# Loading two quarters of a weight in column halves, and trying more plans, in a fused attention and MoE kernel that plans its own instruction order

## The chip, the cores and the metric

The kernel runs on 1 core of one Trainium2 chip. The metric is device time in microseconds (us).

PE is TensorE (PEld its weight loads), DVE is VectorE, ACT is ScalarE, POOL is GpSimd, SP is SyncE.

## The reference, cut to what matters

```python
# q, k, v: (8 batches, 8 heads, 576, 64) float32; attention in a window of +-32 positions
scores = where(abs(i - j) <= 32, q @ k.T / 8, -1e9)
attn_out = softmax(scores) @ v
x = attn_out.transpose(0, 2, 1, 3).reshape(4608, 512)     # one row per token
h = x @ w_in            # (512, 2048)
g = relu(h) ** 2
out = g @ w_out         # (2048, 512), float32 out
```

## The kernel before

The kernel is a generator. It records every operation with what it reads and writes, an estimated duration and a key; then it plans an order for all five engines with a model of its own, several times over with different offsets, keeps the plan that its model likes best, and emits that order with the semaphore waits that it needs. So a change of the loads also changes the order of everything else.

The tokens are worked in 9 tiles of 512. For the first tile the first product is cut into 16 units: token group g (128 tokens) by weight quarter q (512 of the 2048 columns of w_in). A unit is 16 matmuls of 128 columns. It may start when the attention result of its group and its quarter are there.

```python
MORE = (-1000, -500, 0, 500, 1000, 1500)          # offsets that are tried on modelled landings
ORDER = ("k01 q01 v00 v01 v02 k03 q03 v03 k04 q04 w10 w11 v04 w12 w13 k05 q05 k10 q10 v10 k11 q11 v11 "
         "w20 w21 w22 w23 k12 q12 v12 k13 q13 v13 k14 q14 v14").split()    # POOL's loads, in order

def load_w1(self, d, key):                        # a quarter of w_in, float32 in HBM, cast to bf16
    src = self.w_in[:, 512 * d:512 * d + 512].rearrange("(f p) c -> p f c", p=128)
    self.p.rec("POOL", lambda e: e.dma_start(self.W1[:, :, 512 * d:512 * d + 512], src),
               writes=[("w1", d)], dma=(f"w1{d}", 0), key=key, dur=770, move=(32, 82, 500 if d > 1 else 1300))

def mm1_small(self, T, g, q, key):                # one unit of the first product
    ...
    def f(e):
        for d in range(4 * q, 4 * q + 4):
            for ft in range(4):
                mm = e.matmul(ht[:, 128 * (d % 4):128 * (d % 4) + 128], self.W1[:, ft, 128 * d:128 * d + 128],
                              self.XT[:, ft, t0:t0 + 128], start=(ft == 0), stop=(ft == 3))
        return mm
    first = self.p.rec("PE", f, reads=[("xt", 8 * T + 2 * g), ("xt", 8 * T + 2 * g + 1), ("w1", q)],
                       writes=[("ht", k % 2), ("mo", k)], key=key, dur=900)
    ...

def mm2(self, T, u, seg, key):                    # second product: a quarter (seg) of w_out, one output bank
    x = 4 * T + u
    gt, op, tag = self.GT[T % 2], self.OUTP[x % 2][:], ("outp", x % 2)    # two output banks in all
    ...                                           # reads ("w2", seg)

# schedule(): for every offset in MORE and every margin, plan; keep the best by the model
    for pad, more in [(p, m) for p in PADS for m in MORE]:
        ...
        if best is None or s < best[0]:
            best = (s, out, start, end, T)
```

A name like `w10` is quarter 0 of w_in, `w23` is quarter 3 of w_out, `v04` is piece 4 of v of batch 0, `k12` is piece 2 of k of batch 1. All these loads cast float32 to bf16 and go through one queue, that of POOL.

The softmax here doesn't subtract the row's maximum and nothing guards it: scores larger than these inputs give would overflow.

## Time and profile before

| | before |
|---|---|
| device time, median of 3 runs | 299.93 us (299.88 to 300.82) |
| span of the profiled run | 297.6 us |
| PE busy | 289.7 us, 97% |
| packets in POOL's queue | 113120 |
| first MoE matmul | 17.37 us |
| last w_out quarter lands / is first used | 41.1 / 41.4 us |

A line of the timeline has the start, the duration, the engine, the line of the kernel, the operation and its operands; in brackets is how long the engine idled before and what ended that. An issue line of a DMA ends with the microseconds from issue to landing.

### The profile page before, as it was taken

What the parts mean: (1) busy time and instruction counts of PE and PEld (TensorE: products, weight loads), DVE (VectorE), ACT (ScalarE), POOL (GpSimd) and SP (SyncE); (2) the same over time, 40 slices, a digit from 0 to 9 for tenths busy, and PEclk for the clock granted to TensorE, in tenths of its full rate; (3) what the DMA queues carried; (4) which work ended last, traced back from release to release, by engine and by line L of the source; (5) the groups of instructions that cost most, each with busy time, mean ns of one, the idle gap of its engine ahead of it and who ended that gap; (6) DMA issues with size and microseconds to landing.
All of it is one profiled execution on the core that took longest, in us unless ns stands there. A gap on an engine that the chain in (4) does not pass through costs nothing.

```text
span 297.6 us, 6577 instructions
## 1 busy us (share of the span) xinstructions
PE 289.7 (97%) x2669; PEld 167.1 (56%) x2705; DVE 174.9 (59%) x407; ACT 160.9 (54%) x265; POOL 105.7 (36%) x131
## 2 busy tenths in 40 slices
PE   8989999999999999999999999999999999999996
PEld 4679855867678754454444454545454544444445
DVE  4865764774989974787565756845554862222200
ACT  2856534657668646573656465546564654444411
POOL 8999841432435514540445424325410000000000
PEclk9999999999999999999999999999999999999999
DMA  9999999999999999999999999999993030100122
GB/s 156 169 201 169 207 172 193 177 157 157 160 175 187 128 183 144 143 150 158 149 109 164 160 151 133 108 171 121 166 119 98 9 82 36 37 35 35 37 89 88
DMA packets 166814, 39.30 MB, mean 132 GB/s; under 512 B 157824, under 2 KB 162304, under 8 KB 166784
## 3 DMA queue, kind: packets, MB, share of 16 engines
q0 software_dynamic: 113120, 17.90, 90.5%
q1 hardware_dynamic: 46512, 11.15, 27.8%
q10 hardware_dynamic: 7152, 9.83, 9.6%
q8 instruction: 21, 0.34, 0.4%
q14 instruction: 9, 0.07, 0.1%
HBM read 36.70 MB, written 9.44 MB: 155 GB/s over the span
## 4 chain that ended last, share of the span: by engine, by line
PE 89%; POOL 4%; DMA 4%; issue 1%; ACT 0%; DVE 0%; POOLq 0%
PE outp L935 40%; PE ht L883 28%; PE ht L865 7%; PE ht L842 5%; DMA qraw<-in_q_dram 4%; PE sc L719 3%; PE sc L663 3%; POOL vx L546 1%; POOL kraw L480 1%; POOL w L568 1%; PE sc L506 1%; POOL qraw L480 1%; PE sc L911 1%; PE outp L911 1%; PE sc L767 0%
## 5 line engine op out<-in xcount | busy, mean ns | idle before, releaser
L935 PE MATMUL outp<-w,gt 128*128 128x512 bf16 x535 | 132.0, 379 | 1.6 <-issue 0.5
L898 DVE TENSOR_TENSOR gt<-rt 128x512 bf16<-128x512 bf16 x144 | 59.5, 419 | 63.4 <-ACT rt L889 55.5
L883 PE MATMUL ht<-xt,w 128*128 128x512 bf16 x373 | 93.4, 379 | 0.8 <-issue 0.2
L889 ACT ACTIVATE rt<-ht 128x512 bf16<-128x512 f32 x96 | 57.2, 599 | 61.3 <-PE ht L883 58.8
L935 PEld LDWEIGHTS outp<-w,gt 128*128 128x128 bf16 x560 | 53.0, 98 | 59.2
L883 PEld LDWEIGHTS ht<-xt,w 128*128 128x128 bf16 x384 | 36.4, 98 | 41.5
L480 POOL DMA_DIRECT2D qraw<-in_q_dram x39 | 34.3, 881 | 50.9 <-PE ht L883 28.1
L480 POOL DMA_DIRECT2D kraw<-in_k_dram x39 | 34.4, 882 | 38.2 <-PE ht L883 18.7
L546 POOL DMA_DIRECT2D vx<-in_v_dram x40 | 35.7, 894 | 23.2 <-PE ht L883 10.7
L942 ACT ACTIVATE oe<-outp 128x512 f32<-128x512 f32 x35 | 20.9, 598 | 28.1 <-PE outp L935 28.1
L684 ACT ACTIVATE e<-sc 128x1024 bf16<-128x1024 f32 (+1 forms) x38 | 31.7, 875 | 7.3 <-PE sc L663 7.3
L700 DVE TENSOR_TENSOR pt<-e,mask 128x512 bf16<-128x512 bf16 (+1 forms) x63 | 29.6, 507 | 9.4 <-ACT e L684 9.1
L743 DVE TENSOR_TENSOR xr<-pf,rs 128x512 bf16<-128x512 f32 (+1 forms) x42 | 27.4, 681 | 0.3
L842 PE MATMUL ht<-xt,w 128*128 128x128 bf16 x384 | 23.9, 219 | 0.8 <-DMA w<-in_moe_w_in_dram 0.8
L865 PE MATMUL ht<-xt,w 128*128 128x256 bf16 x192 | 23.3, 273 | 0.0
L842 PEld LDWEIGHTS ht<-xt,w 128*128 128x128 bf16 x384 | 21.7, 98 | 1.5 <-DMA w<-in_moe_w_in_dram 0.9
L736 DVE COPY pf<-sc 128x520 f32<-128x520 f32 x21 | 14.7, 698 | 8.9 <-PE sc L719 8.6
L865 PEld LDWEIGHTS ht<-xt,w 128*128 128x128 bf16 x192 | 17.9, 98 | 3.1 <-DMA xt<-xr 0.2
L850 ACT ACTIVATE rt<-ht 128x512 bf16<-128x512 f32 x24 | 14.3, 598 | 9.5 <-PE ht L842 9.2
L738 DVE TENSOR_TENSOR pf<-pf 64x520 f32<-64x520 f32 x21 | 14.7, 698 | 5.9 <-ACT pf L733 5.2
L733 ACT ACTIVATE pf<-sc 128x520 f32<-128x520 f32 x21 | 12.6, 601 | 9.6 <-PE sc L719 8.9
L871 ACT ACTIVATE rt<-ht 128x512 bf16<-128x512 f32 x24 | 14.4, 599 | 6.3 <-PE ht L865 5.0
(85 smaller groups left out, 174.7 us busy)
## 6 DMA issues: line engine op xcount, KB each, us to landing
out_dram<-oe ACTq DMA_DIRECT2D x35, 256.0 KB, 2.9
kraw<-in_k_dram POOLq DMA_DIRECT2D x30, 128.0 KB, 5.2
qraw<-in_q_dram POOLq DMA_DIRECT2D x30, 128.0 KB, 5.2
vx<-in_v_dram POOLq DMA_DIRECT2D x24, 128.0 KB, 5.5
w<-in_moe_w_in_dram POOLq DMA_DIRECT2D x4, 512.0 KB, 10.2
w<-in_moe_w_out_dram POOLq DMA_DIRECT2D x4, 512.0 KB, 16.5
vx<-in_v_dram POOLq DMA_DIRECT2D x16, 96.0 KB, 5.6
xt<-xr SPq DMA_TRANSPOSE x36, 4.0
```

The source lines that it names most:

```text
L480: self.p.rec("POOL", lambda e: e.dma_start(dst, src), writes=[("fraw", b, t, x)], old=[("fraw", b - 2, t, y + (b == 2))], reads=self.pace( ...
L546: self.p.rec("POOL", lambda e: e.dma_start(self.VX[b % 2][r:r + n, s, :, 0:64], self.v[b, :, t0:t0 + n, :].rearrange("h p d -> p h d")), w ...
L684: self.p.rec("ACT", lambda e, d=dst, a=src: e.activation(d, a, ACTF.Exp, scale=0.125), reads=["s" + x for x in ("AC", "BD")[h]], writes=[( ...
L700: self.p.rec("DVE", lambda e: e.tensor_tensor(pt, ee, mb, ALU.mult), reads=[("e", g // 2)] + rd, writes=[("ptt", k)], old=old, key=key + k ...
L743: self.p.rec("DVE", lambda e, w=w, np=np: e.tensor_tensor(bass.AP(self.XR, 512 * (2 * y + w), [[2048, np], [64, 2], [128, 4], [1, 64]]), b ...
L842: mm = e.matmul(ht[:, 128 * (d % 4):128 * (d % 4) + 128], self.W1[:, ft, 128 * d:128 * d + 128], self.XT[:, ft, t0:t0 + 128], start=(ft == ...
L865: mm = e.matmul(ht[:, 256 * (d % 2):256 * (d % 2) + 256], self.W1[:, ft, 128 * d:128 * d + 128], self.XT[:, ft, 64 * s0:64 * s0 + 256], st ...
L883: mm = e.matmul(ht[:], self.W1[:, ft, 128 * d:128 * d + 128], self.XT[:, ft, 512 * T:512 * T + 512], start=(ft == 0), stop=(ft == 3))
L889: self.p.rec("ACT", lambda e: e.activation(rt[:], ht[:], ACTF.Relu), reads=[("ht", k % 2)], writes=[("rt", k % 4)], key=key, dur=560)
L898: self.p.rec("DVE", lambda e: e.tensor_tensor(g, r, r, ALU.mult), reads=[("rt", k % 4)], writes=tags, key=key, dur=430)
L935: mm = e.matmul(op, gt[:, d, 128 * u:128 * u + 128], self.W2[:, d, :], start=(d == 0), stop=(d == 15))
L942: self.p.rec("ACT", lambda e: e.activation(oe[:], op, ACTF.Copy), reads=[tag], writes=[("oe", x % 4)], key=key, dur=560)
```

## The change

Its intent: the first unit waits 0.9 us for quarter 0 of w_in. Loaded in two halves of 256 columns, the first half is there earlier, and the units of the first two token groups are cut so that 8 of their 16 matmuls can run on it. The set of offsets that the planner tries grows from 6 to 13.

```diff
+CUT = 2
-MORE = (-1000, -500, 0, 500, 1000, 1500)
+MORE = (-1500, -1000, -750, -500, -250, 0, 250, 500, 750, 1000, 1250, 1500, 2000)
     def load_w1(self, d, key):
-        src = self.w_in[:, 512 * d:512 * d + 512].rearrange("(f p) c -> p f c", p=128)
-        self.p.rec("POOL", ... writes=[("w1", d)], dma=(f"w1{d}", 0), key=key, dur=770, move=(32, 82, 500 if d > 1 else 1300))
+        parts = 2 if d < CUT else 1
+        w = 512 // parts
+        for h in range(parts):
+            lo = 512 * d + w * h
+            src = self.w_in[:, lo:lo + w].rearrange("(f p) c -> p f c", p=128)
+            self.p.rec("POOL", ... writes=[("w1", d, h)],
+                       dma=(f"w1{d}{h}", 0), key=key + 0.4 * h, dur=770, move=(32, 82, 500) if parts == 1 else (32, 43, 1300))
     # mm1_small
+        if T == 0 and q < CUT and g < 2:
+            for h in range(2):
+                op = self.p.rec("PE", lambda e, h=h: f(e, range(4 * q + 2 * h, 4 * q + 2 * h + 2)), reads=xs + [("w1", q, h)],
+                                writes=[("ht", k % 2)] + ([("mo", k)] if h else []), key=key, dur=450)
     ...                                  # the other readers wait for both halves
```

More of the change, by code (lines that the diff above doesn't have):

```diff
@@ L566, in load_w1 @@
     def load_w1(self, d, key):
-        src = self.w_in[:, 512 * d:512 * d + 512].rearrange("(f p) c -> p f c", p=128)
-        self.p.rec("POOL", lambda e: e.dma_start(self.W1[:, :, 512 * d:512 * d + 512], src),
-                   writes=[("w1", d)], dma=(f"w1{d}", 0), key=key, dur=770, move=(32, 82, 500 if d > 1 else 1300))
+        parts = 2 if d < CUT else 1
[3 more added lines that the diff above has]
+            src = self.w_in[:, lo:lo + w].rearrange("(f p) c -> p f c", p=128)
+            self.p.rec("POOL", lambda e, lo=lo, src=src: e.dma_start(self.W1[:, :, lo:lo + w], src), writes=[("w1", d, h)],
+                       dma=(f"w1{d}{h}", 0), key=key + 0.4 * h, dur=770, move=(32, 82, 500) if parts == 1 else (32, 43, 1300))
     def load_w2(self, d, key):
@@ L837, in mm1_small, with f @@
         t0 = 512 * T + 128 * g
-        def f(e):
-            for d in range(4 * q, 4 * q + 4):
+        def f(e, ds):
+            for d in ds:
                 for ft in range(4):
@@ L844, in f @@
             return mm
-        first = self.p.rec("PE", f, reads=[("xt", 8 * T + 2 * g), ("xt", 8 * T + 2 * g + 1), ("w1", q)], writes=[("ht", k % 2), ("mo", k)], key=key,
-                   dur=900)
-        if not k:
-            self.p.first = first
+        xs = [("xt", 8 * T + 2 * g), ("xt", 8 * T + 2 * g + 1)]
+        if T == 0 and q < CUT and g < 2:
+            for h in range(2):
+                op = self.p.rec("PE", lambda e, h=h: f(e, range(4 * q + 2 * h, 4 * q + 2 * h + 2)), reads=xs + [("w1", q, h)],
+                                writes=[("ht", k % 2)] + ([("mo", k)] if h else []), key=key, dur=450)
+                if not k and not h:
+                    self.p.first = op
+        else:
+            op = self.p.rec("PE", lambda e: f(e, range(4 * q, 4 * q + 4)), reads=xs + [("w1", q, h) for h in range(2 if q < CUT else 1)],
+                            writes=[("ht", k % 2), ("mo", k)], key=key, dur=900)
+            if not k:
+                self.p.first = op
         self.p.rec("ACT", lambda e: e.activation(rt[:], ht[:], ACTF.Relu), reads=[("ht", k % 2)],
@@ L867, in f @@
             return mm
-        self.p.rec("PE", f, reads=[("xt", s0 + u) for u in range(4)] + [("w1", q // 2)], writes=[("ht", k % 2), ("mo", k)],
+        self.p.rec("PE", f, reads=[("xt", s0 + u) for u in range(4)] + [("w1", q // 2, h) for h in range(2 if q // 2 < CUT else 1)], writes=[("ht", k % 2), ("mo", k)],
                    key=key, dur=870)
@@ L885, in f @@
             return mm
-        self.p.rec("PE", f, reads=[("xt", 8 * T + j) for j in range(8)] + [("w1", d // 4)], writes=[("ht", k % 2), ("mo", k)],
+        self.p.rec("PE", f, reads=[("xt", 8 * T + j) for j in range(8)] + [("w1", d // 4, h) for h in range(2 if d // 4 < CUT else 1)], writes=[("ht", k % 2), ("mo", k)],
                    key=key, dur=854)
```

## The prediction

> **What bounds the kernel now.** I read the page first, then the windows table, then the timeline of the first 44 us, then the issues of the weight loads one at a time. First the page:
>
> ```profile
> span 297.6 us, 6577 instructions
> PE 289.7 (97%) x2669; PEld 167.1 (56%) x2705; DVE 174.9 (59%) x407; ACT 160.9 (54%) x265; POOL 105.7 (36%) x131
> ...
> DMA  9999999999999999999999999999993030100122
> ...
> q0 software_dynamic: 113120, 17.90, 90.5%
> ...
> PE 89%; POOL 4%; DMA 4%; issue 1%; ACT 0%; DVE 0%; POOLq 0%
> ```
>
> PE is busy in 97% of the span and carries 89% of the chain of waits; only a DMA and the load issues on POOL take its place, and only early. So the end moves if PE idles less or starts real work sooner, nothing else. The windows table (stretch, length, busy time of PE, PEld, DVE, ACT, POOL) says where PE idles:
>
> ```profile
> 13.40:17.37 3.97, 2.91 (x72) 2.07 (x65) 3.40 (x10) 3.02 (x4) 3.97 (x7) 1.00 1.25 207
> 17.37:20.00 2.63, 2.44 (x45) 2.30 (x46) 1.17 (x3) 1.26 (x3) 2.63 (x4) 1.00 1.52 193
> 20.00:26.50 6.50, 6.34 (x117) 6.13 (x118) 3.65 (x9) 4.36 (x8) 6.50 (x9) 1.00 1.65 187
> 26.50:36.00 9.50, 9.45 (x166) 8.81 (x166) 6.70 (x18) 5.65 (x11) 8.92 (x11) 1.00 1.63 190
> 36.00:50.00 14.00, 13.89 (x138) 7.51 (x140) 7.89 (x17) 5.53 (x10) 5.26 (x6) 1.00 1.94 189
> ```
>
> Before 17.37 PE idles 3.97 - 2.91 = 1.06 us and also runs fillers on zeros (0.53 and 0.38 us). From 20 to 50 it idles 0.16 + 0.05 + 0.11 = 0.32 us in all. From 50 to 250 the same view sums to about 2.1 us, and some of that is missing matmul records (535 of 560 for the second matmul). So about 2 us could be had before 20 us and about 2 us in the other 230.
>
> The timeline shows what the early wait is for (start, duration, engine, line, operation; idle time and its releaser in brackets):
>
> ```profile
> 9.68 1.57 POOL L568 DMA_DIRECT2D w<-in_moe_w_in_dram  x2
> ...
> 16.38 0.38 PE L430 MATMUL outp<-zz 128*128 128x512 bf16 x1
> ...
> 17.36 0.90 PEld L842 LDWEIGHTS ht<-xt,w 128*128 128x128 bf16 x16 [0.92 <-DMA w<-in_moe_w_in_dram]
> ...
> 19.98 1.05 PE L842 MATMUL ht<-xt,w 128*128 128x128 bf16 x16 [0.19 <-DMA w<-in_moe_w_in_dram]
> ...
> 40.54 2.75 PE L935 MATMUL outp<-w,gt 128*128 128x512 bf16 x12
> ...
> 42.46 0.60 ACT L942 ACTIVATE oe<-outp 128x512 f32<-128x512 f32 x1 [1.12 <-PE outp L935]
> ```
>
> The first MoE unit starts when quarter 0 of w_in lands (17.3 us) and the third when quarter 1 lands (19.8 us). Then the issue lines for single loads, the first w_in quarter and the last w_out quarter (the last column is us from issue to landing):
>
> ```profile
> w<-in_moe_w_in_dram POOLq DMA_DIRECT2D x1, 512.0 KB, 7.6
> ```
>
> ```profile
> w<-in_moe_w_out_dram POOLq DMA_DIRECT2D x1, 512.0 KB, 19.2
> ```
>
> Issued at 9.68, quarter 0 lands at 9.68 + 7.6 = 17.28. In the same way the other w_in quarters land at 19.8, 23.0 and 25.6. The w_out quarters, issued at 19.71, 20.45, 21.19 and 21.93 with 13.8, 15.6, 17.5 and 19.2 us to landing, come at 33.5, 36.1, 38.7 and 41.1. POOL issues in 0.75 us what the queue needs 2.6 us to move, so the queue is a backlog up to 42 us.
>
> That last landing matters most. The 12 matmuls at 40.54 are three groups of four, 0.86 us each: w_out quarter 2 for one token block, then quarter 3 for two. The first use of quarter 3 is therefore at 40.54 + 0.86 = 41.4 us, 0.3 us after it lands. The ACT line agrees: its result is evacuated at 42.46, after PE has finished at about 42.3. In the same way quarters 0, 1 and 2 are used 1.9, 1.3 and 0.7 us after they land. The slack shrinks along the row: **PE runs into the queue at 41 us.**
>
> **What the Trainium skill says.** "DMA: Bandwidth & Descriptors", Specifications, gives 512 B as the smallest transfer at line rate. A half quarter has rows of 256 columns, 512 B in bf16: just at that limit. No row of before has that size, so this trace neither agrees nor disagrees; it shows only 1 KB and 128 B packets. The same page, "Issuing engines are not separate DMA queues", says that all issuers share the 16 engines; the backlog of before agrees. The page "TensorE: Matmul & The Clock Gate", "Wait — 56ns, not 53.3ns?", gives 56 ns between 128-column matmuls; the chain shows 0.89 us for 16 of them, 56 ns. So a half unit of 8 is 0.45 us.
>
> **The change part by part.** (1) Two loads of 512 KB become four of 256 KB. PE now waits for halves, and the units of token groups 0 and 1 with quarters 0 and 1 are each recorded as two halves of 8 matmuls. No matmul is added or removed; four more PE waits and two more POOL issues are. POOL: 2 x 0.75 = 1.5 us more of issuing, all in front of a backlog of 7 to 19 us, so it reaches nobody.
>
> (2) The queue. Between 14.5 and 17.2 us only weights moved: 547 packets in 2.7 us on 16 engines, 79 ns for one of 1 KB. Between 17.5 and 19.8 us, 772 small and 334 large packets moved: 2300 - 334/16 x 79 = 650 ns for 48 small ones per engine, 13.5 ns each. A straight line through 128 B at 13.5 and 1 KB at 79 gives an overhead of some 4 ns a packet. Halving turns 512 packets per quarter into 1024, 32 more per engine: 32 x 4 = 0.13 us a quarter, 0.26 us for two. This estimate takes 512 B to be on that line. All later loads of the queue land 0.26 us later: w_out quarter 3 at about 41.4 us. The queue's count should be 113120 + 1024 + 2 x 16 = 114176, the 32 being completion packets (126 issues x 16 = 2016 account for what the data rows leave over).
>
> (3) The first units. Half 0 of quarter 0 should land at 17.28 - 1.31 + 0.07 = 16.05, half 1 at 17.4, the halves of quarter 1 at 18.8 and 20.1. Laying out PE with the measured pieces (transposes 0.25, attention 0.25, half 0.45): unit 0 half 0 at 16.1, in what was filler and idle time; half 1 from 17.4 to 17.85; transpose and attention to 18.4; unit 1 to 19.3; half 0 of units 2 and 3 to 20.2; their other halves to 21.1; attention to 21.4. Before, unit 3 ended at 21.15 + 0.90 = 22.05. **PE is 0.65 us ahead at 21 us.**
>
> (4) Whether it keeps it. Everything PE can do before w_out quarter 3 is used up in before: all 16 first-tile units (256 matmuls by 35.3), six of eight w_out groups for the two open output banks, and the attention of the first rows of batch 1. The next inputs (k and q of batch 1, piece 2) were issued at 22.66 and land 19.3 us later, at 42. There are only two output banks, so the other token blocks cannot open. So the 0.65 us becomes waiting at 41 us: PE may pass there min(0.65, 0.3 - 0.26) = 0.04 us sooner. If the packet overhead turns out zero it is 0.3.
>
> (5) The plans. The generator lays the instructions out with its own model and keeps the best of a set; the offsets grow from 6 to 13 and contain the old six, so in its own measure it cannot lose by this. On the chip it can choose among orders whose real idle after 42 us is at most 2 us. I put this at -0.25 us, with some 0.7 us of scatter either way, since any other order meets other DMA landings; this one number is judgement.
>
> Sum: 299.93 - 0.04 - 0.25 = 299.6 us.
>
> **The rivals.** (a) The head start is kept: 0.65 us early, the new order finds filling work at 41 us, and the time is 299.93 - 0.65 - 0.25 = 299.0. For it: PE idles almost nothing after 20 us, and a wholly PE-bound program keeps what it gains. Against it: the 0.3 us at w_out quarter 3. (b) The smaller packets are dear: if a 512 B packet costs nearly what one of 1 KB does, the queue loses 2 x 2.6 = 5 us and the second half lands at 20, so PE stalls from 17 to 46 us: 303 to 305. Against it: 128 B packets at 13.5 ns. (c) A new plan is worse on the chip than in the model, say a late activation load or transpose that PE waits for: 300.5 to 301.5. For it: loads of later batches are paced by PE's progress, and DMA is at 9 tenths for 30 slices. (d) POOL's 1.5 us counts: then v, k and q pieces land later, q piece 5 at 26.0 first (PE already waited 0.15 us for it), about 300.3. Against it: those loads lie behind weights.
>
> **Range and chances.** Weights: the central case 50%, (a) 25%, (c) and (d) 22%, (b) 2%. The range for 8 in 10 is 298.7 to 300.7: its low end is (a) with a lucky plan, its high end (c) at its mildest. Two per cent are 6 us. Faster by that would need 294 us, which is more than all idle time found; 0.01. Slower needs (b) or an unlucky plan; 0.02. Within: 0.97.
>
> **What would show it.** Step 2: the packet count, and w_out quarter 3 landing 0.2 to 0.3 us later than the 41.1 us here. Step 3: first MoE matmul at 16.1 rather than 17.37, and the filler in front of it gone. Step 4: PE idle between 34 and 42 us, some 0.5 us more than before, with a w_out load as releaser; if instead 42 us is reached with no wait and earlier, (a) holds. Step 5: idle after 50 us unlike the 2.1 us here. A first landing near 17 us, or idle of several us between 17 and 30, would make (b) right. A difference that lies after 60 us would say that the order chosen, not the halves, decided the time.

## More of the kernel before

Most lines that carry the argument are in the prediction and not shown twice. Four more are needed later: a copy of a piece of v on DVE, the fourth and fifth unit, the start of the second product, and the first unit of the second tile.

```profile
20.55 0.29 DVE L563 COPY vd<-vx 64x528 bf16<-64x528 bf16 x1 [1.02 <-DMA vx<-in_v_dram]
...
21.15 1.95 PE L842 MATMUL ht<-xt,w 128*128 128x128 bf16 x32
...
35.39 0.81 PE L935 MATMUL outp<-w,gt 128*128 128x512 bf16 x3
...
51.42 1.05 PE L842 MATMUL ht<-xt,w 128*128 128x128 bf16 x16
```

## The result, and the profile after

| | before | after |
|---|---|---|
| device time, median (same rounds) | 299.90 us (299.74 to 300.82, 4 runs) | 299.63 us (299.56 to 300.07, 4 runs) |
| ratio after / before, 95% interval | | 0.9988 (0.9966 to 1.0010) |
| span of the profiled run | 297.6 us | 297.8 us |
| packets in POOL's queue | 113120 | 114176 |
| first MoE matmul | 17.37 us | 16.12 us |
| w_in lands (halves: 0a, 0b, 1a, 1b) | 17.3, 19.8 | 15.3, 17.4, 18.7, 20.04 |
| last w_out quarter lands / is first used | 41.1 / 41.4 us | 41.5 / 41.57 us |
| first unit of the second tile | 51.42 us | 51.61 us |

The ratio is the mean time of the fast runs of one kernel over that of the other's of the same rounds, so it is not quite the ratio of the medians.

The page of the changed kernel, the lines that answer to those of before (span, busy time, the queue, the chain by engine):

```profile
span 297.8 us, 6575 instructions
...
PE 288.8 (97%) x2669; PEld 166.1 (56%) x2704; DVE 173.9 (58%) x407; ACT 161.1 (54%) x265; POOL 106.5 (36%) x133
...
q0 software_dynamic: 114176, 17.90, 89.8%
...
PE 82%; POOL 7%; DMA 6%; DVE 2%; issue 1%; ACT 0%; POOLq 0%
```

The bytes are the same and the packets are exactly 1056 more. PE's share of the chain fell from 89% to 82%, and POOL and DMA took it: the chain now runs through the queue for longer. Its timeline shows where:

```profile
16.12 0.61 PE L847 MATMUL ht<-xt,w 128*128 128x128 bf16 x8
...
17.44 1.51 PE L847 MATMUL ht<-xt,w 128*128 128x128 bf16 x24 [0.46 <-DMA w<-in_moe_w_in_dram]
...
19.25 1.95 PE L847 MATMUL ht<-xt,w 128*128 128x128 bf16 x32
...
20.26 1.04 POOL L547 DMA_DIRECT2D vx<-in_v_dram  x1
...
20.76 0.67 DVE L564 COPY vd<-vx 64x528 bf16<-64x528 bf16 x1 [0.72 <-DMA vx<-in_v_dram]
...
21.48 0.20 PE L799 MATMUL sc<-vd,pt 128*128 128x65 bf16 x1 [0.28 <-DVE vd L564]
...
21.73 3.14 PE L847 MATMUL ht<-xt,w 128*128 128x128 bf16 x48
...
35.17 1.67 PE L948 MATMUL outp<-w,gt 128*128 128x512 bf16 x7
...
39.07 0.55 PEld L948 LDWEIGHTS outp<-w,gt 128*128 128x128 bf16 x4 [0.43 <-DMA w<-in_moe_w_out_dram]
...
41.57 1.90 PE L948 MATMUL outp<-w,gt 128*128 128x512 bf16 x8
...
51.61 1.05 PE L847 MATMUL ht<-xt,w 128*128 128x128 bf16 x16
```

Half a unit runs at 16.12, 1.25 us before anything did. (Its half had landed at 15.3; PE came to it only at 16.12, after the attention products that its order puts first.) At 19.25 + 32 x 0.056 = 21.05 us the first four units are done; before, the fourth ended at 22.05, with one more attention product done. Then PE waits for a copy of v that had waited for a load. At 35.17 PE starts the second product, 0.22 us before its old 35.39. And at 41.57, the first use of the last w_out quarter, it is 0.17 us *later* than the old 41.4. The chain of waits of the changed kernel says why; its line is one piece of the chain (start, length, what):

```profile
23.33 18.19 DMA w<-in_moe_w_out_dram
```

The path to 41.5 us is now one load: the last w_out quarter, from its issue at 23.33 to its landing. In before, the piece that stood there was a load landing at 26.0 and then PE alone.

The windows table of the changed kernel, for the stretches shown of before:

```profile
13.40:17.37 3.97, 3.16 (x72) 2.34 (x64) 3.29 (x10) 3.05 (x4) 3.97 (x7) 1.00 1.47 197
17.37:20.00 2.63, 2.56 (x50) 2.57 (x51) 1.63 (x4) 1.61 (x3) 2.63 (x4) 1.00 1.62 188
20.00:26.50 6.50, 6.08 (x111) 5.77 (x108) 3.51 (x9) 3.88 (x8) 6.50 (x9) 1.00 1.59 191
```

PE gains 0.25 and 0.12 us of busy time before 20 us and loses 0.26 between 20 and 26.5: it waits 0.28 us for the copy of v and 0.14 us at 23.8 for a w_in quarter. (The last three numbers of a line are the granted clock, the DMA share and the GB/s.)

### The profile page after: what moved, and what is told of

The parts are those of the page before. It is cut to its first block, busy times and chain, and to the rows that moved or that the text cites. A ratio compares the mean times of both kernels' runs of the same rounds, so it can differ in the third digit from the quotient of the medians.

```text
span 297.8 us, 6575 instructions
## 1 busy us (share of the span) xinstructions
PE 288.8 (97%) x2669; PEld 166.1 (56%) x2704; DVE 173.9 (58%) x407; ACT 161.1 (54%) x265; POOL 106.5 (36%) x133
## 3 DMA queue, kind: packets, MB, share of 16 engines
q0 software_dynamic: 114176, 17.90, 89.8%
## 4 chain that ended last, share of the span: by engine, by line
PE 82%; POOL 7%; DMA 6%; DVE 2%; issue 1%; ACT 0%; POOLq 0%
PE outp L948 38%; PE ht L896 28%; DMA w<-in_moe_w_out_dram 6%; PE ht L878 6%; PE sc L724 3%; PE sc L668 3%; PE ht L847 3%; POOL vx L547 2%; POOL kraw L481 2%; POOL qraw L481 2%; POOL w L573 1%; POOL w L578 1%; PE sc L924 1%; PE outp L924 1%; DVE pf L743 0%
## 5 line engine op out<-in xcount | busy, mean ns | idle before, releaser
L896 PEld LDWEIGHTS ht<-xt,w 128*128 128x128 bf16 x384 | 36.5, 98 | 42.3 <-DMA xt<-xr 0.3
```

What stands on the lines that cost most here:

```text
L896: mm = e.matmul(ht[:], self.W1[:, ft, 128 * d:128 * d + 128], self.XT[:, ft, 512 * T:512 * T + 512], start=(ft == 0), stop=(ft == 3))
```

## The experiments

The question was where the head start goes. **Queue theory:** POOL's queue delivers in order and PE consumes nearly as fast up to 42 us, so a head start turns into waits for whatever lands next, in the end for the last w_out quarter. **Rivals:** the new instruction order loses it (the planner), or the difference lies elsewhere and the landing at 41 us holds nothing.

One thing was settled with no run. The planner's own record of its trials was printed for the changed kernel: the plan that it kept has offset -500, which is among the old six. Built with the old set, the changed kernel has the same instructions in the same order on all five engines. So **the wider set does nothing in the changed kernel**; all of the change is the halves. Runs of that kernel and of the changed one are therefore repeats of one program.

Twelve runs were made, on three chips; each is compared with runs of before. All gave correct results. Medians and, in brackets, the ratio to before with its 95% interval.

### e1: the wider set alone, loads whole

```diff
-MORE = (-1000, -500, 0, 500, 1000, 1500)
+MORE = (-1500, -1000, -750, -500, -250, 0, 250, 500, 750, 1000, 1250, 1500, 2000)
```

> One part alone: the kernel before with the 13 candidate offsets, loads whole. Its generator picks offset 750 instead of 0, which its own model puts 0.08 us better. Queue theory (the w_out quarters bound PE at 41 us): first MoE matmul still at 17.4 us, w_out quarter 3 lands at 41.1, nothing to gain: 299.6 to 300.1 us. Rival (the order chosen is what decides): a difference of 0.5 us or more in either direction, seen as idle of PE after 50 us.

Measured: 299.73 us against 299.84 (1.000, 0.9981 to 1.0019). The first MoE matmul stayed at 17.3 us, and no w_out load was waited for. The plan is another one, offset 750, and the time is the same. The profiled run was one of its slower ones (span 298.7 us); the waits from 60 to 150 us in it name the reason:

```profile
PE ht L883 <- DMA xt<-xr: 0.8, 1, 0.8
```

A single wait for a transpose by DMA, 0.8 us. The trace of before has no PE wait for a transpose in that stretch. This run took 1.0 us longer than before from the second tile to the end, and the wait is most of that. The scatter is wide for what is studied here: 38 runs of before in all lie between 299.31 and 303.33 (the last one with a granted clock of 0.994).

### e2: the halves alone, old set (a repeat of the changed kernel)

```diff
-MORE = (-1500, -1000, -750, -500, -250, 0, 250, 500, 750, 1000, 1250, 1500, 2000)
+MORE = (-1000, -500, 0, 500, 1000, 1500)
```

> The other part alone: halves, with the six old offsets. Compared before the run, its instruction order is the same as that of the changed kernel on all five engines (the winner is offset -500, which was among the old six), so this is also a repeat of the changed kernel: 299.6 us, first MoE matmul at 16.1, w_out quarter 3 at 41.5. Any difference from 299.63 is what runs of one program scatter by.

Measured: 299.75 us against 299.84 (1.0002, 0.9983 to 1.0021). First matmul at 16.19, second tile at 51.74. The repeat differs from the first trace by 0.1 us at these marks.

### e3: the halves in the order of before

```diff
     def schedule(self):
-        ... try offsets and margins, keep the best
+        out = sorted(self.ops, key=lambda o: (place_in_before[o], half))   # order of before, halves side by side
```

> Halves with the order of instructions of the kernel before kept on every engine (each halved load or unit in the place of the whole one). Queue theory: first MoE matmul at 16.1, PE some 0.4 us ahead of before at 22 us, w_out quarter 3 lands 0.4 us later than before at 41.5, PE waits there for it some 0.5 us, and passes 43.3 us 0.1 to 0.2 us later than before; 299.9 to 300.2 us. Rival (the head start of the changed kernel was lost to its new order, at 21 to 26 us): here the head start is kept past 42 us and the time is 299.3 to 299.6.

Measured: 300.04 us against 299.84 (1.0004, 0.9986 to 1.0022). The time is what the queue theory said, but not at the place that it said. The timeline:

```profile
16.47 0.61 PE L817 MATMUL ht<-xt,w 128*128 128x128 bf16 x8
...
20.07 0.62 PE L817 MATMUL ht<-xt,w 128*128 128x128 bf16 x8 [0.24 <-DMA w<-in_moe_w_in_dram]
21.49 0.20 PE L769 MATMUL sc<-vd,pt 128*128 128x65 bf16 x1 [0.80 <-DVE vd L534]
```

PE is ahead at 20.07 and stands 0.80 us at 21.49, for the copy of v that needs `v04`, the load right behind the halved w_in quarters. `v04` landed at 20.69 and the copy took 0.72 us, where before took 0.29: 0.43 of the 0.80 us is the slow copy, not the load (see point 3 below). There was no wait at 41 us, since PE came there late (second product from 35.77, against 35.39). The rival's forecast, 299.3 to 299.6, did not come: with the order of before, the head start is lost even earlier. What takes it is not the w_out landing but this copy, which came late by the queue and then ran slowly.

### e4: all four w_in quarters in halves

```diff
-CUT = 2
+CUT = 4
```

> The suspected cost doubled: all four w_in quarters in halves. 115232 packets in the queue (113120 + 4 x 512 + 4 x 16). If the packet overhead delays what is behind it, w_out quarter 3 lands 0.4 us later than in the changed kernel, at 41.9 to 42.0, and PE waits more for it: 299.8 to 300.2 us. If the 0.4 us that the changed kernel showed is not the packets, it stays at 41.5 and the time at 299.6.

Measured: 299.85 us against 299.84 (0.9999, 0.9982 to 1.0017), 115232 packets as counted ahead. The last w_out quarter was issued at 24.8 and landed 17.0 us later, at 41.8 (41.9 to 42.0 was expected), 0.3 us after that of the changed kernel, and PE waited for it by name:

```profile
41.87 1.90 PE L948 MATMUL outp<-w,gt 128*128 128x512 bf16 x8 [0.33 <-DMA w<-in_moe_w_out_dram]
```

One landing scatters by some 0.2 us, so all traces with this order of loads count: with none halved 41.14 and 41.30 (before, e1), with two 41.47 to 41.65 (changed, e2, e3, e9), with four 41.82. The means rise by 0.33 and 0.60 us, for 64 and 128 more packets per DMA engine: about 5 ns each. The prediction's straight line had 4 ns, which this scatter cannot tell from 5. The direction, later with more packets, is plain.

### e5: the last w_out quarter one load later, nothing else

The order of the changed kernel was frozen on every engine; on POOL, `w23` and `k12` change places.

```diff
-    ... w20 w21 w22 w23 k12 q12 ...
+    ... w20 w21 w22 k12 w23 q12 ...        # order on PE, DVE, ACT, SP unchanged
```

> One wait made longer, nothing else: the changed kernel with its order kept on PE, DVE, ACT and SP (compared: the same), and on POOL the last w_out quarter issued behind one k load instead of before it. That load takes 64 x 13.5 ns = 0.86 us of the queue, so quarter 3 lands at 41.5 + 0.9 = 42.4 us. Queue theory (PE is held at 41.5 us by this landing): PE passes 0.9 us later and stays so to the end: 299.7 + 0.9 = 300.6 us. Rival (this landing holds nothing, PE has other slack): 299.7 us as before.

Measured: 300.49 us; before 299.98 (1.0021, 0.9996 to 1.0046). The interval holds 1, and the changed kernel medians are 299.63, 299.75 and 299.73, so the step costs some 0.75 to 0.85 us. They were run at other times. The trace is plainer than the time. The quarter was issued at 24.21 and landed 18.1 us later, at 42.3:

```profile
42.33 1.90 PE L948 MATMUL outp<-w,gt 128*128 128x512 bf16 x8 [0.99 <-DMA w<-in_moe_w_out_dram]
...
44.07 0.39 PE L507 MATMUL sc<-identw,kraw 128*128 128x128 bf16 x4
```

PE passes 0.76 us later than in the changed kernel (42.33 against 41.57), the second tile starts at 52.36 instead of 51.61, and the last matmul group at 294.59 instead of 293.54. The landing is 0.77 us later, and so, within 0.02 us, are PE's passing and the second tile; the last 0.3 us at the end are scatter (see after e12). This is the cleanest run: **in the changed kernel the last w_out quarter holds PE, and what PE loses there is not made good.**

### e6: the kernel before, with the w_out quarters one load earlier

```diff
-... k11 q11 v11 w20 w21 w22 w23 k12 ...
+... k11 q11 w20 w21 w22 w23 v11 k12 ...        # planned anew
```

> Control: the kernel before (whole loads) with the v load of the second piece of batch 1 issued behind the w_out quarters instead of before them; its generator plans anew. w_out quarter 3 lands 0.8 us earlier, at 40.3. Queue theory: PE comes to it at 41.4 anyway and gains at most the 0.3 us of other small waits: 299.6 to 300.0 us, no change. Rival (the queue alone sets the time up to 41 us, whatever PE does): 299.1.

Measured: 300.17 us against 299.98 (1.0004, 0.9981 to 1.0028). The quarter landed at 40.4, 0.7 us earlier, and the second tile started at 51.77, 0.35 us later than in before. So the earlier landing brought nothing, as expected, but the run does not show why. The v load that was moved back now landed at 41.24, PE stood 0.2 us before an attention product with v at 41.37, and it came to quarter 3 at 41.62 instead of 41.40. That PE would not have been there yet is not shown by this run.

### e7 and e11: the halves, with the w_out quarters one load earlier

The same edit on the changed kernel, planned anew. e11 is e7 once more: both traces have the same instructions in the same order on all engines.

> Halves, with the same v load behind the w_out quarters, planned anew: quarter 3 lands at 40.7. Queue theory: PE's head start of 0.2 to 0.3 us at 35 us now survives 41 us, and the waits of 0.7 us on w_out there go: 43 us is passed 0.4 to 0.6 us sooner than in the changed kernel, 299.1 to 299.4 us. Rival (the head start is lost elsewhere, or the new plan costs as much): 299.7.

> The halves with one v load behind the w_out quarters, repeated beside the changed kernel: its second tile should again start at 50.7 us against 51.6, and its time be 0.2 to 0.6 us below that of the changed kernel on this chip (299.2 to 299.5).

In the trace the expectation is met in both runs. The quarter lands at 40.5 (e11: 40.7); the wait for w_out shrinks to 0.2 us on the weight loads (0.3); and in e7 by 43.54 PE has done 36 matmuls of the second product, where the changed kernel has done 32 by 43.32. Four of them take 0.86 us, so PE is 0.86 - 0.22 = 0.6 us ahead of the changed kernel. Of that, 0.2 us was there at 35 us already (second product from 34.94, against 35.17). The second tile:

```profile
50.72 1.06 PE L847 MATMUL ht<-xt,w 128*128 128x128 bf16 x16
```

That is e7; e11 has 50.87, against 51.61 in the changed kernel.

The times do not follow: both medians missed the expected range. e7: 299.56 us against 299.98 (0.9992, 0.9965 to 1.0019), with a lowest run of 299.00. e11, beside the changed kernel: 300.48 against the changed kernel's 299.73, with runs from 299.42 to 301.13. In e11 four of six runs were above 300.3; the profiled one (299.56, span 297.7) has a PE wait for a transpose of 0.3 us where e7 has none. So in all its traces this version carries the head start past 43 us, and then loses part of it or all of it later: e11 was 0.74 us ahead of the changed kernel's trace at the second tile and level with it at the end. 5 of its 12 runs are above 300.2 us, against 2 of 16 of the changed kernel. Why its later part scatters more, its order being a different one, stays open. It is not shown to be a better version.

### e8: one more v load moved back

```diff
-... k10 q10 k11 q11 w20 w21 w22 w23 v11 ... (after v10)
+... k10 q10 k11 q11 w20 w21 w22 v10 w23 v11 ...
```

> As the run before with one more v load (96 rows, 0.65 us of the queue) moved behind the third w_out quarter; the order on PE, DVE, ACT and SP is the same as in the run before (compared), so only landings differ. Quarter 3 lands at 40.7 too (both v loads: one behind it, one just in front), quarters 0 to 2 land 0.65 us earlier. If PE waits on any of quarters 0 to 2 there: up to 0.2 us faster; if on quarter 3 alone: the same as the run before within 0.1 us; if the moved v load is now late for the attention products of batch 1: slower.

Measured: 300.04 us against 299.98 (1.0001, 0.9975 to 1.0027). The marks are those of e7 (second tile at 50.74, last group at 293.23 against 292.98): no gain from earlier quarters 0 to 2, so in this order none of them held PE.

### e9: the changed kernel again

No edit; beside e10 to e12.

> The changed kernel once more, beside the three runs that follow, so that they are compared on one chip: 299.6 to 299.8 us, within 0.1% of the kernel before. First MoE matmul 16.1 us, the first unit of the second tile at 51.6 us, w_out quarter 3 at 41.5 us.

Measured: 299.73 us against 300.23 (0.9982, 0.9964 to 1.0000). Marks 16.3, 51.64 and 41.6, as expected. Its time is that of the other repeats. That it be within 0.1% of before was missed: before was slower, 6 of its 11 runs being above 300.2.

### e10: the kernel before, with the last w_out quarter one load later

The edit of e5 on the kernel before.

> The kernel before, its order kept on PE, DVE, ACT and SP, the last w_out quarter issued behind one k load: it lands at 41.1 + 0.85 = 41.95 us. Before had 0.3 us between this landing and its use at 41.4, so PE should be held 0.55 to 0.6 us, with the landing as releaser, less than the 0.75 to 1.0 us that the same step cost the changed kernel: before + 0.55 us. If it costs the full 0.85, the 0.3 us of slack that the prediction read from the profile was not there.

Measured: 300.27 us against 300.23 (1.0003, 0.9985 to 1.0021). Inconclusive in time, since before scattered as much as the effect. In the trace, the quarter landed at 42.1 and PE waited for it:

```profile
42.18 1.90 PE L935 MATMUL outp<-w,gt 128*128 128x512 bf16 x8 [0.19 <-DMA w<-in_moe_w_out_dram]
```

The matmuls before it started at 40.96, so the group ended at 40.96 + 0.86 = 41.82 and PE stood 0.36 us; but in this run PE was 0.4 us late already at 35.8 (the first landing came 0.17 us later, and the copy of v took 0.76 us for 0.29). 0.36 + 0.4 is 0.76 us of landing delay that PE would have met at the old 41.4. That fits a slack of 0.2 to 0.3 us for 1.0 us of delay; it does not show it cleanly.

### e12: both waits moved

e7, and `v04` issued ahead of the last w_in half.

```diff
+        at["v04"] = at["w11"] + 0.2      # between the two halves of quarter 1
```

> As the run before, and the v load that PE waited for at 21.5 us (0.28 us in the changed kernel) issued in front of the last w_in half instead of behind it. It lands at 19.4 instead of 20.7, the half 0.65 us later at 20.7. If the wait at 21.5 was what took the rest of the head start, PE is another 0.1 to 0.3 us ahead at 36 us: 299.0 to 299.4 us. Rival (the later half costs as much as the earlier v load gives): as the run before.

Measured: 300.17 us against 300.23 (0.9999, 0.9982 to 1.0016), second tile at 52.25: the rival's case, and worse. The wait at 21.5 is gone, a wait of 0.17 us for the w_in half takes its place, and the v load that had been moved back is now the one that PE lacks:

```profile
PE sc L724 <- DMA vx<-in_v_dram: 0.7, 1, 0.7
```

Here, and by its marks in e6, the reordering moved the wait to another load of the queue.

### From the second tile to the end, over all traces

From the first unit of the second tile to the end of the last matmul, six of the fourteen traces take 243.85 to 243.88 us (before, changed, e2, e4, e10, e12). The other eight take 244.2 to 244.8, e7, e8 and e11 among them. None takes less. So a head start or a delay at the second tile goes through to the end, and in eight traces 0.3 to 1.0 us came on top. One of these eight is e9, the changed program again, with 244.2.

## Why the prediction was right or wrong, point by point

The time was right: 299.6 predicted, 299.63 measured, inside the range. The interval of the ratio is some 0.7 us wide to either side, so it cannot tell the forecast gain of 0.3 us from none. Not every step was right.

**What bounds the kernel: right.** PE up to the end, the queue up to 42 us. For the changed kernel e5 shows it in the trace: 0.77 us of landing became 0.75 us at the second tile. In time the same step is 0.75 to 0.85 us.

**(1) The parts: right but for one.** There is no matmul more and there are two issues more. In the queue POOL's 1.5 us of issuing reached nobody: the load of q piece 5 landed at 26.21 for 26.02, so rival (d) fell. But POOL's issues were shifted, and one of them lay over the copy of v at 20.76 (point 3).

**(2) The queue: right, and its size within the scatter.** The count was exact. These are the transfers from 14.5 to 17.2 us, before and after:

```profile
DMA packets 547, 0.56 MB, mean 207 GB/s; under 512 B 16, under 2 KB 546, under 8 KB 546
```

```profile
DMA packets 1040, 0.53 MB, mean 197 GB/s; under 512 B 33, under 2 KB 1039, under 8 KB 1039
```

Without the small completion packets and one of another queue, which the prediction counted among its 547, 530 of 1 KB and 1006 of 512 B moved in 2.7 us on 16 engines: 81.5 and 42.9 ns each. Two halves cost 85.9 - 81.5 = 4.4 ns more than one whole, so the straight line's 4 ns held at 512 B. The last w_out quarter was predicted 0.26 us later; it was 0.38 in this pair, 0.33 by the means under e4, 0.24 from e6 to e7 and e11, and 0.16 from e10 to e5. The dear-packet rival (b), 5 us, fell. (That no row of before has 512 B is true of POOL's queue. The page of before counts 162304 - 157824 = 4480 packets from 512 B to under 2 KB, 384 more than the 4096 weight rows.)

**(3) The first units: right until 21 us.** Halves were predicted at 16.05, 17.4, 18.8 and 20.1; they landed at 15.3, 17.4, 18.7 and 20.04. The first matmul came at 16.12 for a predicted 16.1, but not because of the landing: the half lay there for 0.8 us. In e2 and e9, the same program, it landed at 16.15 and 16.23 and PE started at once.

What the layout left out is the copy of `v04` on DVE. The load landed 0.2 us later than before (20.73, 20.52), and the copy took 0.67 us for 0.29. It ended at 21.43. At 0.29 us it would have ended at 21.05, and the attention product would have ended near the predicted 21.4 (an estimate). It ended at 21.73, and the head start was 22.05 - 21.73 = 0.32 us instead of 0.65.

The traces show what goes with a slow copy. Each has six copies of this shape, 84 in all. 21 took 0.29 us. The other 63 took 0.31 to 0.85 us, and every one of them ended 0.12 us after the DMA issue of POOL in which it had begun. In the changed kernel that is the issue from 20.26 to 21.30. The 21 began at most 0.21 us after the start of such an issue, or so near its end that 0.29 us outlasted it. In before the copy began 0.09 us into an issue. In e10, with the instructions of before but for one swap on POOL after 21 us, it began 0.27 us into one and took 0.76. So the quick copy of before was luck of 0.1 to 0.2 us, and POOL's issues hold such a copy. That is read from the regularity; no run moved an issue for this alone.

**(4) Whether it keeps it: the mechanism was right, and the sizes were off.** Of 0.32 us some 0.22 were left at 35 us. From there to the first use of the last w_out quarter PE does the same work in both traces. It took 41.40 - 35.39 = 6.01 us in before and 41.57 - 35.17 = 6.40 in the changed kernel. The 0.39 us more are waits for w_out, as forecast (0.5): 0.10 us at 39.07 for quarter 2, which the prediction did not name and which had landed at 39.03, and 0.27 us at 41.3 for quarter 3. The busy time of the windows hides them: 5.84 us of 6.00 in 36 to 42 us, against 5.95. The predicted passing was 0.04 us sooner than before; it was 0.17 later in this pair of traces, the landing being 0.38 us later and the slack 0.26. Rival (a), that the head start is kept, fell; e7 and e11 show that more of it would have been kept past 43 us had that quarter come earlier.

**(5) The plans: wrong.** The wider set was credited with 0.25 us. It changed nothing: the kept plan is in the old set. In e1 it did choose another plan, and the time was 1.000 of before. The halves did bring another order, but from the second tile to the end the two traces take the same 243.85 and 243.88 us, so rival (c), that the new order loses later, is not seen in this pair either.

So the closeness of the sum is luck, by terms that do not each hold: the trace pair is 0.2 us later (span 297.8 against 297.6), the medians 0.27 us earlier. With the changed program (the first, e2 and e9, 16 runs) its mean was 0.37 us below, 0.06 above and 0.50 below that of before. That the program is truly faster is not shown; each interval reaches 1. What these runs suggest, no more, is that it has fewer slow runs: 2 of 16 above 300.2 us against 14 of 38 for before.

## What to carry to other kernels

A load that is waited for early can be cut so that its first half comes sooner, but where one queue feeds everything that follows, the head start is paid back at the next load that the queue holds: read the slack between landing and first use of each later load, and the smallest of them is what the cut can be worth. Count what the cut adds to the queue as well, since more packets delay all that is behind. Look also at what the added issues lie over: here a DVE copy that began more than 0.21 us into a POOL issue ended only after it. And before crediting a wider search, look whether it chose anything that the narrower one did not have.

## What the Trainium skill lacked or had wrong

- "DMA: Bandwidth & Descriptors", Specifications, gives 512 B as the smallest transfer at line rate. The traces bear this out nearly: from 14.5 to 17.2 us 197 GB/s moved in rows of 512 B and 207 in rows of 1 KB (of bf16, cast from float32), some 4 ns for each packet added. There was no cliff at 512 B.
- "SBUF — State Buffer", Who interferes with whom, says that a DVE copy in a 2-port mode and GpSimd exclude each other, and that the one that issues second blocks fully. These traces agree, if this copy (64x528, bf16) ran in such a mode, which they do not tell. They add the size on the DVE side: 0.29 us alone, up to 0.85 us behind a DMA issue of POOL, ending 0.12 us after the issue in 63 of 63 cases. It was enough to halve a head start.
- No page read for this tells how far the landings of one load scatter from run to run, nor how far waits for a DMA transpose do. Here the first half landed at 15.3, 16.15 and 16.2 us in three traces of one program, and a PE wait for a transpose of 0.3 us stood in e11 and not in e7, again one program. Both are as large as the effect studied, or larger.
